# Attention scores on 64 partitions from batch 2 on, the missing rows moved by SBUF to SBUF copies, and GpSimd's value work placed half a group earlier

## The chip, the cores and the metric

The kernel runs on one core of one Trainium2 chip. The metric is the device time of one execution in microseconds (us), lower is better. "Span" is the time from the first to the last instruction of the one execution that was profiled; it is about 2 us below the device time of the same execution (329.5 and 331.33 us before).

## The reference, cut to what matters

```python
# 8 batches, 8 heads, 576 positions, head size 64; q, k, v are 0.1 * randn
def _attn_ref(q, k, v):
    q_d, k_d, v_d = (mean of each 4 neighbouring positions, for q, k and v)
    out_up = np.repeat(softmax(scale * q_d @ k_d.T) @ v_d, 4, axis=2)
    mask = np.abs(pos[:, None] - pos[None, :]) < 4
    scores = np.where(mask, scale * q @ k.T, -1e9)
    return out_up + softmax(scores) @ v

def _moe_ref(x, w_in, w_out):          # x: 4608 tokens x 512, 512 -> 2048 -> 512
    h = x @ w_in
    return (h * (1 / (1 + np.exp(-1.702 * h)))) @ w_out
```

So each batch has a narrow attention inside a band, an attention on pooled positions, and the sum of both goes through a large two-layer network.

## The kernel before: the parts that matter

The 4608 tokens go through the network in nine groups of 512. Group g runs on TensorE as 64 large matmuls with `w_in` and 64 with `w_out`; between fixed ones of them stand the small matmuls of the attention of batch g + 1. There are two score blocks to a batch (`qd` 0 and 1, four heads each), each followed by the scores on pooled positions. GpSimd makes what these blocks need: pooled q and k (`pool_qk`), values cast to bf16 (`prep_v`), pooled values (`prep_v4`). GpSimd also issues the loads of q, k and weights; the SyncE queue issues the value loads and the output stores.

```python
def prep_1(name, b, qd):               # VectorE transposes q or k, 576 columns as 18 x 32
    store, dst = {"k": (kf, kT), "q": (qf, qT)}[name]
    tt = work.tile([128, S, 2], BF16, ..., bufs=1)
    t32 = tt.rearrange("p t a -> p (t a)").bitcast(FP32)
    nc.vector.transpose(out=..., in_=store[b, qd].bitcast(FP32)...)   # pairs of bf16 as one fp32
    dst[b, qd] = tt

def scores(b, qd, barred=False):       # 80 matmuls a block, each on 32 partitions
    ...
    for i in range(5):
        for a in range(2):             # the two elements of a pair, summed in PSUM
            for par in range(2):
                for r in range(4):     # head
                    rows = slice(32 * r, 32 * r + 32)
                    nc.tensor.matmul(sp[r // 2][...],
                        lhsT=kT[b, qd][rows, k0 : k0 + 64, a],
                        rhs=qT[b, qd][rows, q0 : q0 + 60, a],
                        start=(a == 0 ...), stop=(a == 1 ...), tile_position=(32 * r, 64 * par))

for g in range(n_groups):              # what is prepared during group g
    b = g + 1
    ...
    elif b < B:
        if b > 2:
            load_v4(b)
        prep_qk(b, 0); pool_qk(b, 0)
        if b + 1 < B:
            for qd in range(NQ):
                load_qk(b + 1, qd)     # GpSimd issues the next batch's q and k
        prep_v(b, nc.gpsimd)
        if b + 1 < B:
            load_v(b + 1)
        prep_qk(b, 1); pool_qk(b, 1)
        prep_v4(b, nc.gpsimd)
    ...                                # then the attention steps and the group's matmuls
```

The transpose moves pairs of bf16 values. So a head's 64 features lie on 32 partitions, two to a partition, and a score needs two matmuls, one for each element `a` of the pair.

The softmax here doesn't subtract the row's maximum and nothing guards it: scores larger than these inputs give would overflow.

Of the kernel before, what the change touches and what calls it, by code (L numbers as in the profile page):

```python
# [8 lines left out]
FP32 = mybir.dt.float32  # L9
# [10 lines left out]
def kernel(  # L20
# [9 lines left out]
    nc = tc.nc  # L30
# [8 lines left out]
    inv_sqrt_d = 1.0 / math.sqrt(D)  # L39
    KSTART = (0, 56)  # L40
    QSTART = (0, 60)

    ctx.enter_context(
        tc.manual_schedule(engines={ET.PE, ET.Activation, ET.DVE, ET.Pool, ET.SP})
# [19 lines left out]
    eds = [persist.tile([128, 2, 464], BF16, name=f"ed{i}") for i in range(2)]  # L64
    v4 = persist.tile([128, 3, HP, 4 * D], FP32, name="v4")
    kdT = [persist.tile([128, 160, 2], BF16, name=f"kdT{i}") for i in range(NQ)]

    PA = [psum.tile([128, 2, 512], FP32, name=f"pa{i}") for i in range(3)]
    PM = [psum.tile([128, 512], FP32, name=f"pm{i}") for i in range(2)]
# [2 lines left out]
    def ps_tile(n=None):  # L72
        if n is None:
            n = turn["a"] % 3
            turn["a"] += 1
        return PA[n]
# [44 lines left out]
    def fill():  # L121
        nc.vector.memset(wz, 0.0)
        for t in kdT:
            nc.vector.memset(t[:, SD:160, :], 0.0)
        for t in vbs:
            nc.vector.memset(t[:, :, :, 64:65], 1.0)
        for t in vds:
            nc.vector.memset(t[:, :, :, 64:65], 4.0)
        for t in es:
            nc.vector.memset(t[:, :, 300:304], 1.0)  # L130
        for t in eds:
            nc.vector.memset(t[:, :, 432:464], 1.0)
# [122 lines left out]

    def prep_1(name, b, qd):
        store, dst = {"k": (kf, kT), "q": (qf, qT)}[name]
        tt = work.tile([128, S, 2], BF16, name=f"{name}T{qd}", tag=f"{name}T{qd}", bufs=1)
        t32 = tt.rearrange("p t a -> p (t a)").bitcast(FP32)
        nc.vector.transpose(  # L260
            out=t32.rearrange("p (i c) -> p c i", c=18),
            in_=store[b, qd].bitcast(FP32).rearrange("p (c d) -> p c d", c=18),
        )
        dst[b, qd] = tt

    def prep_qk(b, qd):
        prep_1("k", b, qd)
        prep_1("q", b, qd)

    def pool_qk(b, qd, names="kq"):  # L270
        for name, src in (("k", kT), ("q", qT)):
            if name not in names:
                continue
            sv = src[b, qd].rearrange("p (j f) a -> p j f a", f=4)
            t1 = work.tile([128, SD, 2, 2], FP32, name="pq", tag="pq")
            nc.gpsimd.tensor_tensor(  # L276
                out=t1, in0=sv[:, :, 0:2, :], in1=sv[:, :, 2:4, :], op=ALU.add
            )
            if name == "k":
                dst = kdT[qd][:, 0:SD, :]  # L280
            else:
                t = work.tile([128, SD, 2], BF16, name=f"qdT{qd}", tag=f"qdT{qd}", bufs=1)
                qdT[b, qd] = t
                dst = t
            nc.gpsimd.tensor_tensor(
                out=dst, in0=t1[:, :, 0, :], in1=t1[:, :, 1, :], op=ALU.add
            )

    def prep_v(b, eng, i=slice(0, 5), h=slice(0, H)):
        cp = eng.copy if eng is nc.scalar else eng.tensor_copy  # L290
        cp(out=vbs[b % 2][:, i, h, 0:D], in_=vf[b][:, i, h])  # L291
# [47 lines left out]

    def scores(b, qd, barred=False):  # L340
        sp = [ps_tile(), ps_tile()]
        if barred:
            bar_others(sp)
        for i in range(5):
            for a in range(2):
                for par in range(2):
                    for r in range(4):
                        rows = slice(32 * r, 32 * r + 32)
                        k0 = 114 * i + KSTART[par]
                        q0 = 114 * i + QSTART[par]  # L350
                        nc.tensor.matmul(  # L351
                            sp[r // 2][64 * par : 64 * par + 64, r % 2, 60 * i : 60 * i + 60],
                            lhsT=kT[b, qd][rows, k0 : k0 + 64, a],
                            rhs=qT[b, qd][rows, q0 : q0 + 60, a],
                            start=(a == 0 and not barred),
                            stop=(a == 1 or barred),
                            tile_position=(32 * r, 64 * par),
                            skip_group_check=barred,
                        )
        return sp  # L360

    def scores_d(b, qd, sd=None):
        sd = sd or ps_tile()
        bank = sd if sd is PM else [sd[:, u, :] for u in range(2)]
        for kc in range(3):
            for a in range(2):
                for r in range(4):
                    rows = slice(32 * r, 32 * r + 32)
                    j = r % 2
                    nc.tensor.matmul(  # L370
                        bank[r // 2][64 * j : 64 * j + 64, SD * kc : SD * kc + SD],
                        lhsT=kdT[qd][rows, 48 * kc : 48 * kc + 64, a],
                        rhs=qdT[b, qd][rows, :, a],
                        start=(a == 0), stop=(a == 1),
                        tile_position=(32 * r, 64 * j),
                    )
        return sd
# [325 lines left out]
    POS = [13, 16, 33, 42, 53, 62, 71]  # L703
    POS_0 = [16, 18, 27, 54, 68, 60, 76]
    VDP_0 = 52

    o, y, x = {}, {}, {}

# [93 lines left out]
    def loads_2():  # L802
        load_v(2)
        load_v4(2)

    for g in range(n_groups):
        b = g + 1
        if g == 0:
            prep_qk(1, 0)
            pool_qk(1, 0)  # L810
            prep_qk(1, 1)
            load_v(1, gate=after(w_out_bf[0:1, 0, 0:1], nc.vector))
            pool_qk(1, 1)
            nc.gpsimd.tensor_copy(
                out=w_out_bf[0:1, 8, 0:1], in_=vf[1][0:1, 3, 0, 0:1]
            )
            load_w_out(2)
            load_w_out(3)
            for i in range(5):
                prep_v(1, nc.gpsimd, i=slice(i, i + 1))  # L820
            for qd in range(NQ):
                load_qk(2, qd)
            loads_2()
        elif b < B:
            if b > 2:
                load_v4(b)
            prep_qk(b, 0)
            pool_qk(b, 0)
            if b + 1 < B:
                for qd in range(NQ):  # L830
                    load_qk(b + 1, qd)
            prep_v(b, nc.gpsimd)
            if b + 1 < B:
                load_v(b + 1)
            prep_qk(b, 1)
            pool_qk(b, 1)
            prep_v4(b, nc.gpsimd)
        steps = {}
        if b < B:
            for n, f in zip(POS if g else POS_0, attention(b, None if g else (1, 2))):  # L840
                steps.setdefault(n, []).append(f)
            if g == 0:
                steps.setdefault(VDP_0, []).append(lambda: prep_vd_pe(1, PA[2]))
        gT = new_gT() if g else gT0
        mm1(g, gT, steps, 0 if g else 6)
        mm2(g, gT, {n - 16: f for n, f in steps.items() if n >= 16})
# [30 lines left out]
```

## Time and profile before

| what | before |
|---|---|
| time, median of 3 runs | 329.46 us (328.81 to 330.97) |
| span of the profiled execution | 329.5 us |
| TensorE busy | 308.0 us, 93% |
| first score block of a steady batch, from a big matmul's start to the next one's | 1.47 us |
| second score block, the same | 1.76 to 1.90 us |
| group in which batch 2, 3, 4, 5, 6, 7 is prepared | 35.10, 33.71, 33.53, 33.39, 34.32, 33.39 us |

The last row is worked out from the trace: from the start of a group's first matmul with `w_in` to that of the next group.

First the page of the kernel before: span, busy time of the engines, then the span in 40 slices (tenths of busy time; PEclk is the granted TensorE clock in tenths, DMA the mean busy share of the 16 DMA engines), and the engines of the chain of waits that ended last.

```profile
span 329.5 us, 11220 instructions
PE 308.0 (93%) x4987; PEld 157.9 (48%) x5043; DVE 130.2 (40%) x215; ACT 184.1 (56%) x322; POOL 138.9 (42%) x168
PE   8767999789999999999999999998999999999995
PEclk9997999999999999999999999999999999999999
DMA  7999979999814991398339922993180110011011
PE 87%; issue 4%; SPq 3%; ACT 2%; DVE 2%; DMA 1%; DVEq 0%; ACTq 0%
```

TensorE bounds the kernel, and in this execution its clock never drops after the start-up (mean 0.995; other runs of the same kernel have means from 0.982).

Now the timeline of TensorE in the group of batch 2 (start, length, engine, line, operation, tiles, count).

```profile
79.42 0.84 PE L351 MATMUL pa<-qT,kT 32*64 32x60 bf16 x80
80.06 0.59 PE L370 MATMUL pa<-qdT,kdT 32*64 32x144 bf16 x24
80.59 2.76 PE L618 MATMUL pm<-xT,w_in_bf 128*128 128x512 bf16 x11
...
90.55 0.48 PE L431 MATMUL pa<-vd,ed 48*64 48x65 bf16 x18
```

L431 holds the products with the pooled values. L351 holds the band's scores, L370 the pooled ones; none of these waits. From 79.42 to 80.06 the 80 matmuls start 8 ns apart.

And the timeline of GpSimd in the same group, cut. L285 ends a pooled q or k, L291 is the cast of the values, L300 ends a pooled value.

```profile
73.03 0.67 POOL L285 TENSOR_TENSOR qdT<-pq 128x288 bf16<-128x288 f32 x1
...
75.78 2.36 POOL L291 CAST vb<-vf 128x2560 bf16<-128x2560 f32 x1
...
81.17 0.67 POOL L285 TENSOR_TENSOR qdT<-pq 128x288 bf16<-128x288 f32 x1
...
87.19 0.84 POOL L300 TENSOR_TENSOR vd<-v 112x256 bf16<-112x256 f32 x1
```

The first pooled q is ready at 73.7 us, 6 us before the scores want it, and the last pooled value at 88.0.

### The profile page before, as it was taken

The page shows a single profiled execution, that of the slowest core. Times are in us where ns is not written, and L with a number is a line of the kernel's source. Part 1 is how long each engine was busy: PE and PEld are TensorE (multiplying, and loading weights), DVE is VectorE, ACT ScalarE, POOL GpSimd, SP SyncE. Part 2 cuts the span into 40 slices and gives each one's busy share as a digit, 9 for nine tenths or more (in the row PEclk, how much of TensorE's full clock was granted, in tenths as well). Part 3 has the DMA queues.
Part 4 walks back from the last instruction along what each step waited for, and adds up shares of the span by engine and source line. Part 5 has one row for each costly group of instructions (what it writes and reads, how often), then busy time and mean ns, then how long its engine had stood idle before and what let it go on. Part 6 is the DMA issues. An engine that isn't in the chain of part 4 may idle for free.

```text
span 329.5 us, 11220 instructions
## 1 busy us (share of the span) xinstructions
PE 308.0 (93%) x4987; PEld 157.9 (48%) x5043; DVE 130.2 (40%) x215; ACT 184.1 (56%) x322; POOL 138.9 (42%) x168
## 2 busy tenths in 40 slices
PE   8767999789999999999999999998999999999995
PEld 3444455445554455455544555455444544444444
DVE  4870512770468036802771277225730560000000
ACT  2552773375936683667367746674566646415611
POOL 7890844049603970298029901990098000000000
PEclk9997999999999999999999999999999999999999
DMA  7999979999814991398339922993180110011011
GB/s 126 184 188 208 171 151 183 196 210 236 191 39 132 205 207 39 116 193 171 102 100 200 200 83 86 196 195 105 40 172 2 60 41 32 2 72 56 2 62 65
DMA packets 63552, 41.36 MB, mean 126 GB/s; under 512 B 44048, under 2 KB 54416, under 8 KB 63504
## 3 DMA queue, kind: packets, MB, share of 16 engines
q1 hardware_dynamic: 55056, 26.95, 35.8%
q0 software_dynamic: 8304, 13.63, 23.9%
q8 instruction: 39, 0.64, 0.9%
q14 instruction: 9, 0.07, 0.1%
q10 hardware_dynamic: 144, 0.07, 0.1%
HBM read 44.83 MB, written 9.44 MB: 165 GB/s over the span
## 4 chain that ended last, share of the span: by engine, by line
PE 87%; issue 4%; SPq 3%; ACT 2%; DVE 2%; DMA 1%; DVEq 0%; ACTq 0%
PE pm L618 35%; PE pm L674 33%; PE pa L351 3%; SPq L214 3%; PE pa L618 2%; PE pa L431 2%; PE pa L409 2%; PE pa L370 2%; PE pa L458 2%; PE pa L674 2%; DMA vf<-in_v_dram 1%; PE pm L689 1%; PE pa L484 1%; ACT vd L321 0%; PE pa L312 0%
## 5 line engine op out<-in xcount | busy, mean ns | idle before, releaser
L618 PE MATMUL pm<-xT,w_in_bf 128*128 128x512 bf16 x528 | 120.3, 380 | 1.4 <-DVE xT L561 0.7
L674 PE MATMUL pm<-w_out_bf,gT 128*128 128x512 bf16 x493 | 114.1, 379 | 5.4 <-issue 5.2
L629 ACT ACTIVATE gT<-pm 128x512 bf16<-128x512 f32 x136 | 81.0, 598 | 45.2 <-PE pm L618 45.2
L618 PEld LDWEIGHTS <-w_in_bf 128*128 128x128 bf16 x576 | 55.8, 98 | 68.4 <-issue 2.5
L674 PEld LDWEIGHTS <-gT 128*128 128x128 bf16 x560 | 51.7, 98 | 59.5 <-issue 0.2
L276 POOL TENSOR_TENSOR pq<-kT 128x576 f32<-128x576 bf16 x16 | 18.5, 1157 | 105.0 <-DVE kT L260 96.1
L395 DVE TENSOR_TENSOR es<-es,mask 128x600 bf16<-128x600 bf16 x28 | 20.6, 749 | 92.0 <-ACT es L381 91.2
L659 ACT ACTIVATE osb<-pm 128x512 f32<-128x512 f32 (+2 forms) x35 | 20.7, 592 | 40.2 <-PE pm L674 36.1
L534 ACT COPY od<-pa 128x384 f32<-128x384 f32 (+1 forms) x56 | 18.4, 412 | 32.4 <-DVE y L444 18.7
L444 DVE TENSOR_TENSOR y<-pa,rc 128x896 bf16<-128x896 f32 x32 | 34.9, 1092 | 1.1
L555 DVE TENSOR_TENSOR xT<-pa,od 128x570 bf16<-128x570 f32 x28 | 21.1, 753 | 12.0 <-ACT od L534 11.9
L381 ACT ACTIVATE es<-pa 128x600 bf16<-128x600 f32 x32 | 19.8, 668 | 7.0 <-PE pa L351 6.8
L297 POOL TENSOR_TENSOR v<-v 112x512 f32<-112x512 f32 x18 | 22.8, 1265 | 0.0
L661 DVE TENSOR_SCALAR osb<-pm 128x128 f32<-128x128 f32 x1 | 0.3, 292 | 55.3 <-ACT osb L659 55.3
L260 DVE STREAM_TRANSPOSE kT<-kb 128x576 f32<-128x576 f32 x16 | 20.0, 1249 | 2.0 <-DMA kb<-in_k_dram 2.0
L260 DVE STREAM_TRANSPOSE qT<-qb 128x576 f32<-128x576 f32 x16 | 19.8, 1239 | 0.9 <-DMA qb<-in_q_dram 0.7
L276 POOL TENSOR_TENSOR pq<-qT 128x576 f32<-128x576 bf16 x16 | 18.4, 1148 | 0.0
L291 POOL CAST vb<-vf 128x2560 bf16<-128x2560 f32 (+1 forms) x11 | 17.6, 1618 | 0.0
L442 DVE RECIPROCAL rc<-pa 128x14 f32<-128x14 f32 x32 | 7.7, 240 | 21.7 <-PE pa L431 21.7
L351 PE MATMUL pa<-qT,kT 32*64 32x60 bf16 x1280 | 14.0, 203 | 1.5 <-issue 1.5
L351 PEld LDWEIGHTS <-kT 32*64 32x64 bf16 x1280 | 11.8, 104 | 6.7 <-issue 5.5
L300 POOL TENSOR_TENSOR vd<-v 112x256 bf16<-112x256 f32 x18 | 13.7, 759 | 1.4
(90 smaller groups left out, 247.0 us busy)
## 6 DMA issues: line engine op xcount, KB each, us to landing
vf<-in_v_dram SPq DMA_DIRECT2D x80, 128.0 KB, 4.7
out_dram<-osb SPq DMA_DIRECT2D x35, 256.0 KB, 2.1
v<-in_v_dram SPq DMA_DIRECT2D x36, 192.0 KB, 6.1
kb<-in_k_dram POOLq DMA_DIRECT2D x16, 288.0 KB, 6.8
qb<-in_q_dram POOLq DMA_DIRECT2D x16, 288.0 KB, 7.1
w_out_bf<-in_moe_w_out_dram POOLq DMA_DIRECT2D x4, 512.0 KB, 12.1
w_in_bf<-in_moe_w_in_dram POOLq DMA_DIRECT2D x2, 512.0 KB, 5.7
w_in_bf<-in_moe_w_in_dram POOLq DMA_DIRECT2D x1, 1024.0 KB, 10.7
```

The lines of the kernel that those rows point to most:

```text
L260: nc.vector.transpose(out=t32.rearrange("p (i c) -> p c i", c=18), in_=store[b, qd].bitcast(FP32).rearrange("p (c d) -> p c d", c=18),)
L276: nc.gpsimd.tensor_tensor(out=t1, in0=sv[:, :, 0:2, :], in1=sv[:, :, 2:4, :], op=ALU.add)
L297: eng.tensor_tensor(out=t1[0:112], in0=x[:, :, 0:2, :], in1=x[:, :, 2:4, :], op=ALU.add)
L351: nc.tensor.matmul(sp[r // 2][64 * par : 64 * par + 64, r % 2, 60 * i : 60 * i + 60], lhsT=kT[b, qd][rows, k0 : k0 + 64, a], rhs=qT[b, qd] ...
L381: nc.scalar.activation(out=es[2 * qd + u][:, :, 0:300], in_=sp[u][:, :, 0:300], func=AF.Exp, scale=inv_sqrt_d,)
L395: nc.vector.tensor_tensor(out=ev, in0=ev, in1=mask, op=ALU.mult)
L444: nc.vector.tensor_tensor(out=y, in0=ov[:, :, :, 0:D], in1=rc.to_broadcast([128, 2, 7, D]), op=ALU.mult,)
L555: eng.tensor_tensor(out=sub(xT[hp], t0 + 3, (57, 2), (114, 5), (1, 57)), in0=sub(x, 3, (509, 2), (57, 5), (1, 57)), in1=sub(od, 3, (57, 2) ...
L618: nc.tensor.matmul(acc, lhsT=w_in_bf[:, dmc, ffc * 128 : (ffc + 1) * 128], rhs=xT[dmc][:, g * TG : g * TG + TG], start=(dmc == 0), stop=(d ...
L629: nc.scalar.activation(out=gT[:, ffc, :], in_=acc, func=AF.Silu, scale=GELU_SCALE)
L659: eng.activation(out=osb, in_=ap, func=AF.Copy, scale=1.0 / GELU_SCALE)
L674: nc.tensor.matmul(ops[t], lhsT=gT[:, ffc, t * 128 : (t + 1) * 128], rhs=w_out_bf[:, ffc, :], start=(ffc == 0), stop=(ffc == n_ffc - 1),)
```

## The change

The intent is to halve the score matmuls. From batch 2 on, q and k are transposed twice, and four copies to each tensor, from SBUF to SBUF on the SyncE queue, move 32 partitions and shift by one element, so that the second elements of the pairs stand on the other 32 partitions of a pair of heads. A head's 64 features are then on 64 partitions, and one matmul does what two did. Pooling on GpSimd reads the result, so it waits for the copies too. To give GpSimd room, the value work of batches 3 to 7 is done during the group before or at the start of its own; in batch 2 it stays behind the q and k sums.

```diff
+    ROWS64 = 2
 def prep_1(name, b, qd):
+        n = 2 if b >= ROWS64 else 1
+        tt = work.tile([128, 2, S, 2], BF16, ..., bufs=1)
+        for x in range(n):
+            ... nc.vector.transpose(out=(half x of tt), in_=(as before))
+        if n == 2:
+            for x in range(2):
+                f = tt[:, x].rearrange("p t a -> p (t a)")
+                for r in range(2):
+                    src = 64 * r + 32 * x
+                    to = 64 * r + 32 * (1 - x)
+                    nc.sync.dma_start(
+                        out=f[to : to + 32, 0 : 2 * S - 1], in_=f[src : src + 32, 1 : 2 * S]
+                    )
 def pool_qk(b, qd, names="kq"):
+            if b >= ROWS64:
+                ... (sums over element 0 of both halves; k goes to a new tile kdP)
 def scores(b, qd, barred=False):
+        if b >= ROWS64:
+            ... 40 matmuls, rows = slice(64 * u, 64 * u + 64), start=True, stop=True
+            return sp
 def scores_d(b, qd, sd=None):
+        if b >= ROWS64:
+            ... 12 matmuls on 64 rows
+    V4 = 34
+    def next_v4(b):
+        load_v4(b)
+        prep_v4(b, nc.gpsimd)
 for g in range(n_groups):
         elif b < B:
-            if b > 2:
-                load_v4(b)
+            if g > 1:
+                prep_v(b, nc.gpsimd)
             prep_qk(b, 0)
             pool_qk(b, 0)
             if b + 1 < B:
                 for qd in range(NQ):
                     load_qk(b + 1, qd)
-            prep_v(b, nc.gpsimd)
+            prep_qk(b, 1)
+            pool_qk(b, 1)
+            if g == 1:
+                prep_v(b, nc.gpsimd)
+                prep_v4(b, nc.gpsimd)
             if b + 1 < B:
                 load_v(b + 1)
-            prep_qk(b, 1)
-            pool_qk(b, 1)
-            prep_v4(b, nc.gpsimd)
...
+            if g and b + 1 < B:
+                steps.setdefault(V4, []).append(lambda b=b: next_v4(b + 1))
```

More of the change, by code (lines that the diff above doesn't have):

```diff
@@ L66 @@
     kdT = [persist.tile([128, 160, 2], BF16, name=f"kdT{i}") for i in range(NQ)]
+    kdP = [persist.tile([128, 2, 160], BF16, name=f"kdP{i}") for i in range(NQ)]
     PA = [psum.tile([128, 2, 512], FP32, name=f"pa{i}") for i in range(3)]
@@ L124, in fill @@
             nc.vector.memset(t[:, SD:160, :], 0.0)
+        for t in kdP:
+            nc.vector.memset(t[:, :, SD:160], 0.0)
         for t in vbs:
@@ L257, in prep_1 @@
         store, dst = {"k": (kf, kT), "q": (qf, qT)}[name]
-        tt = work.tile([128, S, 2], BF16, name=f"{name}T{qd}", tag=f"{name}T{qd}", bufs=1)
-        t32 = tt.rearrange("p t a -> p (t a)").bitcast(FP32)
-        nc.vector.transpose(
-            out=t32.rearrange("p (i c) -> p c i", c=18),
-            in_=store[b, qd].bitcast(FP32).rearrange("p (c d) -> p c d", c=18),
-        )
-        dst[b, qd] = tt
+        n = 2 if b >= ROWS64 else 1
+        tt = work.tile([128, 2, S, 2], BF16, name=f"{name}T{qd}", tag=f"{name}T{qd}", bufs=1)
+        for x in range(n):
+            t32 = tt[:, x].rearrange("p t a -> p (t a)").bitcast(FP32)
+            nc.vector.transpose(
+                out=t32.rearrange("p (i c) -> p c i", c=18),
+                in_=store[b, qd].bitcast(FP32).rearrange("p (c d) -> p c d", c=18),
+            )
[7 more added lines that the diff above has]
+                        out=f[to : to + 32, 0 : 2 * S - 1], in_=f[src : src + 32, 1 : 2 * S]
+                    )
+        dst[b, qd] = tt if n == 2 else tt[:, 0]
     def prep_qk(b, qd):
@@ L273, in pool_qk @@
                 continue
+            if b >= ROWS64:
+                sv = src[b, qd].rearrange("p x (j f) a -> p (x j) f a", f=4)[:, :, :, 0]
+                t1 = work.tile([128, 2 * SD, 2], FP32, name="pq", tag="pq", bufs=1)
+                nc.gpsimd.tensor_tensor(
+                    out=t1, in0=sv[:, :, 0:2], in1=sv[:, :, 2:4], op=ALU.add
+                )
+                if name == "k":
+                    dst = kdP[qd][:, :, 0:SD]
+                else:
+                    dst = work.tile([128, 2, SD], BF16, name=f"qdT{qd}", tag=f"qdT{qd}", bufs=1)
+                    qdT[b, qd] = dst
+                t1 = t1.rearrange("p (x j) f -> p x j f", x=2)
+                nc.gpsimd.tensor_tensor(
+                    out=dst, in0=t1[:, :, :, 0], in1=t1[:, :, :, 1], op=ALU.add
+                )
+                continue
             sv = src[b, qd].rearrange("p (j f) a -> p j f a", f=4)
-            t1 = work.tile([128, SD, 2, 2], FP32, name="pq", tag="pq")
+            t1 = work.tile([128, SD, 2, 2], FP32, name="pq", tag="pq", bufs=1)
             nc.gpsimd.tensor_tensor(
@@ L341, in scores @@
         sp = [ps_tile(), ps_tile()]
+        if b >= ROWS64:
+            for j in range(2):
+                for i in range(5):
+                    for par in range(2):
+                        for u in range(2):
+                            rows = slice(64 * u, 64 * u + 64)
+                            k0 = 114 * i + KSTART[par]
+                            q0 = 114 * i + QSTART[par]
+                            nc.tensor.matmul(
+                                sp[u][64 * par : 64 * par + 64, j, 60 * i : 60 * i + 60],
+                                lhsT=kT[b, qd][rows, j, k0 : k0 + 64, 0],
+                                rhs=qT[b, qd][rows, j, q0 : q0 + 60, 0],
+                                start=True, stop=True,
+                                tile_position=(64 * u, 64 * par),
+                            )
+            return sp
         if barred:
@@ L363, in scores_d @@
         sd = sd or ps_tile()
+        if b >= ROWS64:
+            for kc in range(3):
+                for j in range(2):
+                    for u in range(2):
+                        rows = slice(64 * u, 64 * u + 64)
+                        nc.tensor.matmul(
+                            sd[64 * j : 64 * j + 64, u, SD * kc : SD * kc + SD],
+                            lhsT=kdP[qd][rows, j, 48 * kc : 48 * kc + 64],
+                            rhs=qdT[b, qd][rows, j, :],
+                            start=True, stop=True,
+                            tile_position=(64 * u, 64 * j),
+                        )
+            return sd
         bank = sd if sd is PM else [sd[:, u, :] for u in range(2)]
```

## The prediction

> **What bounds it now.** TensorE. The page's busy table has PE at 308.0 of 329.5 us, and the chain of waits is 87% PE instructions; the two big matmul groups take 234 us. Between two big matmuls stand attention blocks. In the timeline a big matmul starts 0.216 us after the last; across the first score block of a batch (80 score and 24 pooled-score matmuls on 32 partitions) the step is 1.47 us, across the second 1.76 to 1.90 us. So a pair costs about 2.9 us. Inside, 80 scores take 0.64 to 0.85 us from start to start, 24 pooled ones 0.37 us: only four different tiles hold these, 6 rounds of 60 ns. The value matmuls, already on 64 partitions, take 9 ns each.
>
> **What the change removes.** In batches 2 to 7, 12 blocks, 52 matmuls of 104. Estimate from the rates above: 40 x 9 ns = 0.36 us, and three rounds of 60 ns = 0.18 us. A block saves 0.45 to 0.6 us: about 6 us, all of it on the critical path. That is just short of 2%.
>
> **What it adds.** 24 transposes of 1.08 us on VectorE, per group in an idle stretch (107 to 119 us of the trace); harmless. 96 DMAs of 74 KB on the SyncE queue, estimated 0.35 to 0.45 us of issue each and about 2 us to landing (the output stores took 2.0). GpSimd's sums keep 576 and 288 elements (1.15 and 0.67 us) but now wait for a DMA as well as a transpose. In the steady groups scores come 11.2 us after the group's start; transposes, DMAs and sums of the first half should take about 10: slack over 1 us. Doing the value sums half a group earlier pays for this on GpSimd.
>
> **Where it is given back: batch 2.** There the value work is still behind the q/k sums. The SyncE queue reuses eight DMA semaphores, so a DMA waits for the eighth before it. Batch 2's first kT copy so waits for a value load that landed at 73.7 us, the qT copies for output stores that landed at 76.2 to 77.8. I expect kT copies landed at 78, qT at 79.5 to 80, the q sum ready at 81.4 instead of 73.64. GpSimd then has the same 14.4 us of work as before (four loads, second q/k sums, the 2.36 us cast, three value sums): done at 95.8, where it was 88.0. PE wants the last pooled values at about 89.8. So PE loses about 6 us in this group: 1.5 to 2 us before its first pooled scores, 4 or more before the pooled value matmuls. A wait that long may also drop the clock: [...] this trace shows 0.5 for 3.41 us after 2.9 us of idle at 23.5. That would add 1 to 1.7 us. Later groups should recover and show only the gain.
>
> **Sum.** 329.5 - 6 + 6 + 1.5 = 331.0 us; range 326 to 335.5. Faster by over 2%: 0.06; within 2%: 0.85; slower by over 2%: 0.09.
>
> **What would show it.** Steps across score blocks of batches 3 to 7 near 1.0 and 1.2 us, and a group near 33 us instead of 34 (right: gain); PE idle 5 to 7 us at 79 to 97 us, released by GpSimd's sums (right: loss); no other PE wait over 1 us in later groups.
>
> **What would make it wrong.** Copies landing faster, or GpSimd's strided sums cheaper: no loss, 323 to 325 us. Copies landing in 4 us or more beside the loads: 1 to 2 us of wait in each group, 336 us or more. Score matmuls bound by loading weights, not by count: half the gain.

The sum: 329.5 - 6 + 6 + 1.5 = 331.0 us, and the 1.5 is an estimate from the trace of the kernel before, 2.87 us of idle up to 26.41 us and then 3.41 us at half rate (27.27 to 30.69), of which half is 1.7. Two other statements can be read there too. SyncE's 153 DMAs use eight semaphores in turn, and 131 of them first wait for the one that they then use. The 24 pooled scores start in six groups of four, about 65 ns from group to group (80.09 to 80.41 us).

## The result, and the profile after

| | before | after |
|---|---|---|
| time, median of 4 runs | 330.0 us (328.81 to 330.97) | 346.53 us (344.53 to 349.16) |
| span of the profiled execution | 329.5 us | 342.7 us |
| batch 2's group | 35.10 us | 49.04 us |
| groups of batches 3 to 7 | 33.71, 33.53, 33.39, 34.32, 33.39 us | 34.02, 33.99, 33.98, 33.17, 32.47 us |
| the two groups after | 27.63, 31.38 us | 27.63, 31.38 us |

The change made the kernel slower: the ratio is 1.0507, with a 95% interval of 1.0427 to 1.0588. Ratios here and below are the mean time of one kernel's fast runs over the mean of the other's fast runs of the same rounds, so they are not quite the ratio of the medians that are quoted. Executions over 1.5% slower than the fastest of the same kernel are left out of the means.

The prediction of 331.0 us and its range up to 335.5 were wrong. The table of groups says where: batch 2's group is 13.94 us longer, and batches 3 to 7 together are 0.71 us shorter (168.34 before, 167.63 after). The sum is 13.2 us, the whole difference of the two spans.

The page after, the same parts as before:

```profile
span 342.7 us, 10264 instructions
PE 307.6 (90%) x4363; PEld 154.5 (45%) x4419; DVE 156.9 (46%) x241; ACT 183.8 (54%) x322; POOL 140.1 (41%) x168
PE   8768998896939898999899989999999999999995
PEclk9998999998778999999999999999999999999999
DMA  7999789895859259875996599859964010011012
PE 50%; DMA 13%; DVE 12%; SPq 8%; issue 6%; POOL 5%; ACT 4%; DVEq 0%; POOLq 0%; ACTq 0%
```

Three things are new. PE has holes in slices 10 and 12 (77 to 86 us and 94 to 103 us), and PEclk falls to 7 and 8 in slices 10 to 13. The DMA row loses its low slices: the copies filled the gaps that the DMA engines had. The chain of waits is now only half TensorE, and DMA, VectorE and the SyncE queue stand in it with a third.

The windows view by group (stretch, its length, then busy time with the number of instructions for each engine, the granted clock, the DMA share and GB/s), first before, batches 2 and 3:

```profile
67.08:102.18 35.10, 33.30 (x594) 17.04 (x600) 17.43 (x27) 21.73 (x39) 17.52 (x19) 1.00 0.74 161
102.18:135.89 33.71, 32.80 (x594) 16.91 (x600) 16.34 (x25) 20.95 (x36) 17.52 (x19) 1.00 0.68 142
```

and after, the same two batches:

```profile
67.09:116.13 49.04, 37.57 (x491) 18.20 (x497) 23.58 (x31) 21.62 (x39) 25.33 (x26) 0.86 0.72 168
116.13:150.14 34.01, 31.74 (x490) 15.99 (x496) 19.70 (x29) 20.95 (x36) 12.95 (x16) 1.00 0.82 173
```

In batch 3's group TensorE has 104 matmuls and 1.06 us of busy time less, as intended, yet the group is not shorter. The DMA engines went from 0.68 to 0.82 there. In batch 2's group the mean clock is 0.86: the clock records show 13.65 us at half rate (82.30 to 89.13 and 99.36 to 106.19).

TensorE's timeline after, batch 2, answers the lines of before; the bracket holds the idle time before the line and what released it:

```profile
83.59 0.57 PE L416 MATMUL pa<-qdT,kdP 64*64 64x144 bf16 x12 [2.08 <-POOL qdT L301]
84.93 4.40 PE L678 MATMUL pm<-xT,w_in_bf 128*128 128x512 bf16 x10 [0.22 <-issue]
...
98.35 0.23 PE L491 MATMUL pa<-vd,ed 48*64 48x65 bf16 x4 [2.00 <-POOL vd L331]
100.37 0.27 PE L491 MATMUL pa<-vd,ed 48*64 48x65 bf16 x4 [1.80 <-POOL vd L331]
102.39 0.38 PE L491 MATMUL pa<-vd,ed 48*64 48x65 bf16 x10 [1.75 <-POOL vd L331]
```

TensorE waits 2.08 us for pooled q, then runs ten big matmuls in 4.40 us (before, eleven took 2.76), and later waits 5.55 us in all for the three pooled values, one after the other.

GpSimd's timeline after, batch 2, cut:

```profile
82.88 0.67 POOL L301 TENSOR_TENSOR qdT<-pq 128x288 bf16<-128x288 f32 x1
...
85.09 0.57 POOL L198 DMA_DIRECT2D qb<-in_q_dram  x1
...
91.43 1.15 POOL L292 TENSOR_TENSOR pq<-qT 128x576 f32<-128x576 bf16 x1 [3.86 <-DMA qT<-qT]
...
93.38 2.56 POOL L322 CAST vb<-vf 128x2560 bf16<-128x2560 f32 x1
...
101.61 0.73 POOL L331 TENSOR_TENSOR vd<-v 112x256 bf16<-112x256 f32 x1
```

The first pooled q is there at 83.5 instead of 73.7. Then GpSimd issues the loads of batch 3's q and k, and the second half's sum waits until 91.43 for its copies. Everything of the value work stands behind that sum. The last pooled value is ready at 102.3 instead of 88.0.

The chain of waits through that place, and through the same place of batch 3's group (start, length, what):

```profile
85.13 6.15 DMA qT<-qT
91.44 1.14 POOL pq L292
...
93.43 2.50 POOL vb L322
...
102.39 0.38 PE pa L491 x10
...
127.01 4.50 DMA qT<-qT
...
134.13 1.42 POOL pq L292
...
136.33 0.38 PE pa L416 x12
```

In batch 2 a copy of the second half took 6.15 us from issue to the sum. In batch 3 the copy issued at 127.01 took 4.85 us to land by the trace, against 2.0 us for the copies of the first half. Between it and the sum at 134.13 the chain goes over ScalarE and VectorE instructions, and the profile names a VectorE mask multiply (L455) as what released the sum. The semaphores in the trace say otherwise: that sum waits only for the transposes, long done, and for the semaphores of four copies. The last copy was issued at 127.60, the last packets of 2,302 bytes, a row of these copies, end at 133.4, and GpSimd's wait for that copy's semaphore ends at 134.0. It was a DMA. Here the wait costs TensorE 1.36 us; the four groups of batches 3 to 6 have 1.36, 1.13, 1.41 and 0.57 us of it, always before L416, and batch 7, which has no following batch to load, has none and takes 32.47 us.

### The profile page after: what moved, and what is told of

Read it like the earlier page. It is cut to its first block, busy times and chain, and to the rows that moved or that the text cites. A ratio compares the mean times of both kernels' runs of the same rounds, so it can differ in the third digit from the quotient of the medians.

```text
span 342.7 us, 10264 instructions
## 1 busy us (share of the span) xinstructions
PE 307.6 (90%) x4363; PEld 154.5 (45%) x4419; DVE 156.9 (46%) x241; ACT 183.8 (54%) x322; POOL 140.1 (41%) x168
## 3 DMA queue, kind: packets, MB, share of 16 engines
q1 hardware_dynamic: 59664, 34.02, 42.3%
## 4 chain that ended last, share of the span: by engine, by line
PE 50%; DMA 13%; DVE 12%; SPq 8%; issue 6%; POOL 5%; ACT 4%; DVEq 0%; POOLq 0%; ACTq 0%
PE pm L734 23%; PE pm L678 14%; DMA qT<-qT 8%; SPq L276 6%; DVE qT L266 4%; DVE kT L266 4%; DMA out_dram<-osb 4%; SPq L218 3%; PE pa L678 2%; PE pa L491 2%; PE pa L469 2%; POOL pq L292 2%; DMA vf<-in_v_dram 2%; PE pa L734 1%; ACT od L594 1%
## 5 line engine op out<-in xcount | busy, mean ns | idle before, releaser
L678 PE MATMUL pm<-xT,w_in_bf 128*128 128x512 bf16 x528 | 122.6, 385 | 1.6 <-DVE xT L621 0.7
L734 PE MATMUL pm<-w_out_bf,gT 128*128 128x512 bf16 x493 | 115.4, 382 | 5.6 <-issue 5.4
L455 DVE TENSOR_TENSOR es<-es,mask 128x600 bf16<-128x600 bf16 x28 | 20.5, 748 | 70.8 <-ACT es L441 70.0
L266 DVE STREAM_TRANSPOSE kT<-kb 128x576 f32<-128x576 f32 x28 | 33.0, 1244 | 2.2 <-DMA kb<-in_k_dram 1.7
L266 DVE STREAM_TRANSPOSE qT<-qb 128x576 f32<-128x576 f32 x28 | 32.8, 1239 | 1.1 <-DMA qb<-in_q_dram 1.1
L292 POOL TENSOR_TENSOR pq<-kT 128x576 f32<-128x576 bf16 x12 | 14.0, 1165 | 33.3 <-DMA kT<-kT 31.7
L292 POOL TENSOR_TENSOR pq<-qT 128x576 f32<-128x576 bf16 x12 | 14.0, 1167 | 19.4 <-DMA qT<-qT 11.9
L491 PE MATMUL pa<-vd,ed 48*64 48x65 bf16 x640 | 12.4, 196 | 6.3 <-POOL vd L331 5.6
L447 ACT ACTIVATE ed<-pa 128x864 bf16<-128x864 f32 x15 | 13.6, 906 | 0.8 <-PE pa L416 0.7
```

What stands on the lines that cost most here:

```text
L266: nc.vector.transpose(out=t32.rearrange("p (i c) -> p c i", c=18), in_=store[b, qd].bitcast(FP32).rearrange("p (c d) -> p c d", c=18),)
L292: nc.gpsimd.tensor_tensor(out=t1, in0=sv[:, :, 0:2], in1=sv[:, :, 2:4], op=ALU.add)
L455: nc.vector.tensor_tensor(out=ev, in0=ev, in1=mask, op=ALU.mult)
L678: nc.tensor.matmul(acc, lhsT=w_in_bf[:, dmc, ffc * 128 : (ffc + 1) * 128], rhs=xT[dmc][:, g * TG : g * TG + TG], start=(dmc == 0), stop=(d ...
L734: nc.tensor.matmul(ops[t], lhsT=gT[:, ffc, t * 128 : (t + 1) * 128], rhs=w_out_bf[:, ffc, :], start=(ffc == 0), stop=(ffc == n_ffc - 1),)
```

## The experiments

Theory A, after the result: the loss is batch 2's, where copies that land late push the value work of the same batch back; the rest of the change is worth what was predicted. Rivals: the new order on GpSimd costs by itself (B); the 96 small issues on one queue are the limit (C). Letters beyond C in the expectations are later forms of the question whether the DMA traffic costs by itself, also where nobody waits for a copy; each says what it expects. Every kernel ran four times, beside seven runs of the kernel before on the same chip; their medians in the four sessions were 331.85, 331.12, 330.11 and 331.68 us. Group lengths are those of the one profiled execution, so small differences between them are not proven. "Waits" are idle times of TensorE.

### 1. Only the order on GpSimd

```diff
-    ROWS64 = 2
+    ROWS64 = 99
```

> Only the new order of GpSimd's work; no batch uses 64 rows, so there is no second transpose and no copy. Theory A (the copies of the second half of q share the DMA engines with the q/k loads of the next batch, land late, and GpSimd's value work of batch 2 stands behind them): without copies nothing is late, 328 to 331 us. Rival B (the new order by itself costs, because in batch 2 the value cast now stands behind the second q/k sums): 335 us or more.

Measured: 332.35 us (332.04 to 332.88), ratio 1.0014 (0.9959 to 1.0068). Groups 36.23, 33.51, 33.39, 35.03, 33.99, 33.39 us. The order by itself costs nothing that can be seen. B falls.

### 2. Everything but the copies

The scores are wrong: half of each matmul's rows belong to another head. The result still passes the comparison, because inputs this small give nearly flat softmaxes, so passing says nothing here.

```diff
-        if n == 2:
+        if n == 3:          # never: no copies
             for x in range(2):
```

> The change without its 96 copies (wrong result on purpose: rows that a copy would fill keep the doubled transpose). Everything else is there: 24 added transposes, 624 fewer matmul pairs, the new order. Theory A and any theory that puts the loss on the copies: the pure gain, 12 blocks at 0.5 us, 323 to 325 us. Rival B, or a loss by the added transposes on VectorE: 330 us or more.

Measured: 329.45 us (326.83 to 330.73), ratio 0.9911 (0.9842 to 0.998). Batch 2's group took 33.97 us with no half clock; where nothing waits a group takes 32.46 us against 33.39 before. So the transposes are harmless, and the gain of 0.93 us a group is real: the 13.94 us and all the waits for GpSimd come with the copies. But the median gained 2.4 us, less than the 5.6 us of six such groups. Two groups of the profiled run hold waits of 1.37 and 1.63 us, which end with no semaphore; experiments 10 and 14 come back to these.

### 3. The next batch's q and k loads behind the pooling

```diff
             prep_qk(b, 0)
             pool_qk(b, 0)
+            prep_qk(b, 1)
+            pool_qk(b, 1)
             if b + 1 < B:
                 for qd in range(NQ):
                     load_qk(b + 1, qd)
-            prep_qk(b, 1)
-            pool_qk(b, 1)
```

> The change, with the q/k loads of the next batch issued after the second q/k sums of this one instead of before. Theory A: the second-half q copies land in 2 to 3 us instead of 5 to 6; in batch 2 GpSimd gets 4 us earlier, the waits of 0.6 to 1.4 us before the second pooled scores of batches 3 to 6 go: 334 to 338 us. Rival C (the cost is SyncE's own issue, 0.6 us for each copy and eight semaphores in turn): unchanged, 343 us or more.

Measured: 347.36 us (347.13 to 351.36), ratio 1.0489 (1.0416 to 1.0562). The expectation of A was missed by 9 us. Its mechanism did show. GpSimd in batch 2, cut:

```profile
84.68 1.15 POOL L292 TENSOR_TENSOR pq<-qT 128x576 f32<-128x576 bf16 x1 [0.70 <-DMA qT<-qT]
...
97.04 0.73 POOL L331 TENSOR_TENSOR vd<-v 112x256 bf16<-112x256 f32 x1
```

The sum that waited 3.86 us for its copies now waits 0.70, and the waits before L416 in batches 3 to 7 are gone but for 0.16 us. But the value work still stands behind all four sums, ends at 97.8 (this execution runs about 2 us earlier, so the gain is about 2 us), TensorE still waits 5.48 us for it, and the clock is at half for the same 13.65 us: batch 2's group is 48.12 us. The later groups took 35.04, 36.81, 36.00, 32.92 and 32.82 us: the loads, moved away from the copies, now run with the value loads, and new waits without a semaphore appear. Moving loads is no cure; it moves the collision.

### 4. Batch 2's value work ahead of its q and k sums

```diff
-            if g > 1:
-                prep_v(b, nc.gpsimd)
+            prep_v(b, nc.gpsimd)
+            if g == 1:
+                prep_v4(b, nc.gpsimd)
             prep_qk(b, 0)
...
-            if g == 1:
-                prep_v(b, nc.gpsimd)
-                prep_v4(b, nc.gpsimd)
```

> The change, with the cast and pooled values of batch 2 ahead of its q/k sums on GpSimd, as in the later batches. If the batch 2 loss is value work that stands behind late copies (theory A, second part), the 8.2 us step before the value matmuls of batch 2 falls to about 1.4 us and the second clock drop goes: 334 to 338 us. If the loss of batch 2 is the first wait alone with the clock that it drops (rival D): 342 us or more.

Measured: 337.79 us (335.68 to 339.24), ratio 1.0168 (1.0104 to 1.0232). TensorE's instructions are the same as after the change. Batch 2's group fell from 49.04 to 40.25 us, with 3.41 us at half clock; no wait for pooled values is left. What is left there are two waits for pooled q:

```profile
84.23 0.58 PE L416 MATMUL pa<-qdT,kdP 64*64 64x144 bf16 x12 [2.12 <-POOL qdT L301]
...
94.49 0.38 PE L416 MATMUL pa<-qdT,kdP 64*64 64x144 bf16 x12 [1.46 <-ACT es L441]
```

The profile puts the second down to ScalarE, but GpSimd's second pooled q, which had waited 4.34 us for its copies, was ready only at 94.44.

So the order of batch 2 is worth 8.8 us, and this was as expected.

### 5. The copies from batch 3 on

```diff
-    ROWS64 = 2
+    ROWS64 = 3
```

> The change with 64 rows from batch 3 on. If the loss is batch 2's (copies that come late behind value loads and stores, value work behind them, half clock after it: its group took 49.0 us against 35.1), this group returns to 35 to 36 us and all else stays: 328.5 to 331 us. If the loss moves to batch 3 with the first use of copies (theory E: any first batch of copies costs it), 336 us or more.

Measured: 336.25 us (333.01 to 338.4; one of the four slow), ratio 1.0122 (1.0049 to 1.0195). Against the change that is 10 us less, and batch 2's group fell from 49.04 to 38.69 us, so most of the loss there came with batch 2's copies. But the expectation was missed twice. The group did not return to 35 to 36 us. With no copy in it, it has a wait of 1.82 us that no semaphore ends, and after that 3.41 us at half clock:

```profile
95.67 0.29 PE L491 MATMUL pa<-vd,ed 48*64 48x65 bf16 x10 [1.82 <-issue]
```

And by A the rest should have been at or below the kernel before, and it is about 4 us above (172.21 against 168.34 us for these five groups): batches 3 to 6 have 1.95, 0.91, 1.36 and 1.81 us of waiting for pooled q, and the last of these is followed by 3.41 us at half clock. The groups of batches 3 to 7 took 34.60, 34.17, 34.74, 36.24 and 32.46 us.

### 6. From batch 3 on, with the later loads

This joins the edits of 3 and 5.

> 64 rows from batch 3 on and the q/k loads of the next batch after the second q/k sums. Later loads took the wait before the second pooled scores away (1.1 to 1.4 us a group) but in the run with them other waits came, 1.5 to 2.7 us each, that no semaphore ends and that follow a landing of PE's own instructions by 1.3 to 1.6 us. If such fetches come late because the q/k loads now meet the value loads (theory F), groups stay at 34 us or more: 330 us or more. If they were chance, groups fall to 32.5 to 33 us: 325 to 327 us.

Measured: 337.87 us (336.33 to 345.43, that one slow), ratio 1.0181 (1.0137 to 1.0224). The waits for pooled q are nearly gone (0.26 us in one group) and the time is no better: waits without a semaphore that add up to 2.65, 1.38, 1.68, 1.71 and 2.18 us stand in the groups of batches 2 to 6. (The profile puts 0.90 us of the 1.68 down to ScalarE; experiment 14 shows why it is counted here.)

### 7 and 8. Half as many copies of twice the size, from batch 2 and from batch 3

```diff
+        if name == "k":
+            pair[qd] = work.tile([128, 2, 2, S, 2], BF16, ...)   # k and q in one tile
+        tt = pair[qd][:, 0 if name == "k" else 1]
-        if n == 2:
+        if n == 2 and name == "q":
...
-                        out=f[to : to + 32, 0 : 2 * S - 1], in_=f[src : src + 32, 1 : 2 * S]
+                        out=f[to : to + 32, :, 0 : 2 * S - 1], in_=f[src : src + 32, :, 1 : 2 * S]
```

> The change with k and q of a half in one tile and one copy for both: 48 copies of 144 KB instead of 96 of 72 KB, the same bytes. Rival C (SyncE's issue, 0.6 us a copy, bounds when copies land): the second half's copies are issued 2 to 3 us earlier, ahead of the q/k loads, the waits before the second pooled scores go in batches 3 to 6, and batch 2 gains 3 us or more: 334 to 340 us. If bytes on the DMA engines bound them: unchanged, 344 us or more.

> Both: 64 rows from batch 3 on and one copy for k and q. If batch 2 and SyncE's issue are the whole loss, five batches keep their gain of 0.95 us each: 324 to 327 us. If bytes bound the copies, as from3: 328.5 to 331 us.

Measured: 347.12 us (346.18 to 351.5), ratio 1.0473 (1.0437 to 1.051), and from batch 3 on 340.79 us (339.81 to 342.95), ratio 1.03 (1.0258 to 1.0343). Half the issues brought no better time from batch 2 on. Batch 2's group did get 3.8 us shorter (45.28 us), as C said, but the waits for pooled q in batches 3 to 6 stayed (0.92, 1.05, 0.67 and 1.04 us), and batch 6's group took 37.62 us, with a wait of 2.38 us without a semaphore and half clock. From batch 3 on it was 4.5 us worse than experiment 5: k's sums wait for q's transposes too, and now even batch 7, with no loads beside it, waits 1.04 us. So fewer issues do not cure the loss. C is not excluded cleanly, because the edit also makes k's copies wait for q's transposes. Both expectations for the second kernel were missed.

### 9. Without the loads of pooled values

The kernel of experiment 6 with `load_v4` left out for batches 3 to 7; its values are wrong (relative error 0.12).

```diff
     def next_v4(b):
-        load_v4(b)
         prep_v4(b, nc.gpsimd)
```

> The kernel from3_later with the v4 loads of batches 3 to 7 left out (wrong result on purpose: these batches pool batch 2's values): PE's instructions are the same to the last, 6 MB of traffic on the DMA engines are gone. Theory F (PE's instruction fetches come late because the DMA engines are full): the fetch waits of 1.4 to 2.7 us in its groups shrink, groups of batches 3 to 7 fall to 32.5 to 33.3 us, 326 to 331 us. Rival G (where the 16 KB instruction blocks happen to end decides, not the traffic): the same waits stay, 336 us or more.

Measured: 335.36 us (329.26 to 335.98). One run counts as fast, the profiled one as slow, so there is no ratio. It did show that the waits without a semaphore are in the same places: 1.66, 2.11 and 2.16 us, before the same counted instructions of TensorE as in experiment 6. Something in the instruction stream fixes the place. But not all is fixed: of the four other waits in the steady groups of experiment 6 (0.83, 1.82, 0.90 and 0.78 us), one fell to 0.72 us and three are gone or under 0.45 us. So three places speak for G and four for F, in one execution of each, and the median lies between the two forecasts.

### 10. The copies' traffic, with nobody reading it

The kernel of experiment 1, plus the change's copies for batches 2 to 7 into an unused half tile.

```diff
+        if b >= 2:
+            f, h = (tt[:, x].rearrange("p t a -> p (t a)") for x in range(2))
+            for x in range(2):
+                for r in range(2):
+                    ... nc.sync.dma_start(out=h[to : to + 32, ...], in_=f[src : src + 32, ...])
```

> The kernel order_only (32 rows everywhere, 332.35 us) with the 96 copies of the change made into a half tile that nothing reads, so no sum and no matmul waits for them: only their traffic and SyncE's issue are added. Theory F: the traffic alone costs, by fetch waits and late loads, 336 to 342 us. Rival H (the copies cost only because GpSimd and PE wait for them): 330 to 334 us.

Measured: 336.02 us (333.51 to 338.12), ratio 1.0157 (1.0069 to 1.0245), against 1.0014 without the copies. The window of batch 3 (columns as above), first without the copies, experiment 1:

```profile
102.01:135.52 33.51, 32.61 (x594) 16.78 (x600) 14.36 (x23) 20.95 (x36) 17.19 (x19) 1.00 0.67 143
```

then with them:

```profile
100.72:137.11 36.39, 33.86 (x602) 17.05 (x601) 15.16 (x25) 20.95 (x36) 21.80 (x24) 1.00 0.86 191
```

Copies that no sum and no matmul waits for cost about 4.7 us (the difference of the ratios, 1.43% of 330; the two intervals just fail to meet, so its size is uncertain by some 3 us). TensorE's program is the same in both; the trace of experiment 1 lacks 56 of TensorE's records, which is why its count here is lower. The DMA share of batch 3's group goes from 0.67 to 0.86, and that group holds a wait of 2.47 us which ends with no semaphore:

```profile
126.44 0.28 PE L500 MATMUL pa<-vd,ed 48*64 48x65 bf16 x8 [2.47 <-issue]
```

Batch 5's group has three such waits, of 0.83, 1.02 and 1.01 us. After the start-up TensorE waits for no sum of GpSimd here. So copies are a cost of their own, apart from anything that waits for them. The run adds their bytes and SyncE's issues together and does not tell the two apart.

### 11. Only the second score block on 64 partitions

Half as many copies, in the order of the kernel before.

```diff
+    def wide(b, qd):
+        return b >= ROWS64 and qd == 1
...
-        n = 2 if b >= ROWS64 else 1
+        n = 2 if wide(b, qd) else 1
(the same in pool_qk, scores and scores_d; value work and loads as in the kernel before, but load_v behind the copies)
```

> 64 rows only in the second half (qd 1) of batches 2 to 7, GpSimd's order as before the change: 12 fewer transposes and 48 fewer copies than the change, which have 8 us more to land. If slack and traffic decide, it keeps most of 6 blocks at 0.5 us and loses nothing in batch 2: 327 to 330 us. If any copies cost more than they give here: 332 us or more.

Measured: 347.93 us (344.37 to 350.07, that one slow), ratio 1.0489 (1.0403 to 1.0575). A clear miss. With the order of before, the value sums of every batch stand behind sums that wait for copies, and so the groups of batches 2 to 6 do what batch 2 does in the change. TensorE's waits for pooled values:

```profile
PE pa L494 <- POOL vd L334: 12.3, 8, 2.0
```

Of the 24 copies whose landing is recorded, 20 land 5.2 to 6.7 us after issue, beside loads, and four groups have 3.41 us at half clock.

### 12 and 13. The same with the value work ahead, from batch 2 and from batch 3

Half the copies as in 11, the order of the change, and in batch 2 the value work before the second half's sums:

```diff
             prep_qk(b, 1)
-            pool_qk(b, 1)
             if g == 1:
                 prep_v(b, nc.gpsimd)
                 prep_v4(b, nc.gpsimd)
+            pool_qk(b, 1)
```

> 64 rows only in the second half as in second_half, but with the change's order: value work a half group ahead from batch 3 on, and in batch 2 before the second q/k sums. In second_half the copies landed 5 to 7 us after issue and GpSimd's value sums stood behind them, so PE waited 2 to 3.5 us for pooled values in each group. If that is the cause, these waits go and 6 blocks keep 0.4 us or more: 328 to 332 us. If copies cost by their traffic whatever stands behind them: 335 us or more.

> The same from batch 3 on, batch 2 with 32 rows: within 2 us of second_ahead if batch 2 is cured there (328 to 332 us); 4 us or more faster if batch 2 still pays.

Measured: 330.41 us (330.25 to 330.65), ratio 0.9962 (0.9914 to 1.0011), and from batch 3 on 331.41 us (330.73 to 333.56), ratio 1.0003 (0.9942 to 1.0064). Both as expected, and both the same as before within the interval. GpSimd in batch 2 of the first, cut:

```profile
74.89 2.37 POOL L325 CAST vb<-vf 128x2560 bf16<-128x2560 f32 x1
...
82.61 0.73 POOL L334 TENSOR_TENSOR vd<-v 112x256 bf16<-112x256 f32 x1
83.30 1.15 POOL L295 TENSOR_TENSOR pq<-kT 128x576 f32<-128x576 bf16 x1
```

The k copies take 6.6 to 6.7 us to land here, yet the sum of k does not wait for them, because 8.4 us of value work stands between; the sum of q waits 0.63 us for the last q copy. It is the order of the value work with its loads, not the speed of a copy, that makes the difference of 17.5 us to experiment 11 (of another session, whose kernel before was 1.6 us faster). No TensorE wait for pooled values is left, only one of 1.36 us for pooled q in batch 2; the groups took 35.24, 32.99, 34.82, 34.45, 33.02 and 32.99 us, and there is no half clock in them. Where nothing waits, half the change gives a little under half the gain (33.39 to 32.99). Two groups lose it again to waits of 1.54 and 1.28 us, which end with no semaphore.

### 14. The same kernel with TensorE's instructions shifted

The waits without a semaphore stood at fixed places. Counted over all of TensorE's records in the trace (matmuls, weight loads and its few semaphore instructions), those of experiment 6, the start-up included, come at 449, 961, 3009, 3265, 4289, 4545, 5313, 6081 and 7105: all leave 193 when divided by 256. The DMA queue that the profile calls "instruction" moves packets of 16 KB (0.64 MB in 39 packets before). Those 39 packets stand beside 10,043 records of TensorE in the same trace, about 257 to a packet. With the remainders this points to one packet for each 256 instructions; below, such a stretch is called a block. So the kernel of experiment 6 got 64 tiny matmuls, 128 instructions with their weight loads, before its first score block:

```diff
     warm(19)
+    t = pm_tile()
+    for _ in range(64):
+        nc.tensor.matmul(t[0:32, 0:8], lhsT=wz[:, 0:32], rhs=wz[:, 0:8], start=True, stop=True)
     make_mask()
```

> from3_later with 64 tiny matmuls (128 PE instructions) put into the wait for the first load. In the traces of from3_later and of no_v4 the waits that no semaphore ends stand before the same PE instructions, 1024 and 1792 (multiples of 256) apart. If PE waits at the ends of its 16 KB instruction blocks (256 instructions), the waits now stand at other lines, 128 instructions earlier in the program, at the same count from its start; the time may move by some us either way. If something else at these lines makes PE wait, they stay at the same lines.

Measured: 332.70 us (332.11 to 333.71), ratio 1.0041 (0.9979 to 1.0103). Adding instructions to the engine that bounds the kernel brought the ratio from 1.0181 down to 1.0041. Two of the waits in TensorE's timeline, first of experiment 6:

```profile
196.68 0.28 PE L491 MATMUL pa<-vd,ed 48*64 48x65 bf16 x8 [1.71 <-issue]
232.79 2.73 PE L734 MATMUL pm<-w_out_bf,gT 128*128 128x512 bf16 x6 [2.18 <-issue]
```

then with the shift:

```profile
201.97 0.21 PE L528 MATMUL pa<-ident,y 48*64 48x48 bf16 x3 [1.84 <-issue]
230.63 0.22 PE L469 MATMUL pa<-vb,es 64*64 64x65 bf16 x2 [1.16 <-issue]
```

The waits stand at other lines but at the same remainder (2241, 4289, 4545, 6593 and 7361 all leave 193). So they come at ends of blocks of 256 instructions, and which stretch of the program has the end decides what it costs. In experiment 3, for example, TensorE resumes 1.4 us after such a packet has ended (packet 137.25 to 138.18, TensorE at 139.60).

The kept traces of experiments 5 to 14, in which no record of TensorE is missing, show more. Their instruction queue moves one 16 KB packet for each block after the first. TensorE never passes a block's start sooner than 1.2 us after the end of its packet (counted in the same way, never sooner than 1.26 us in the trace before and 1.35 us in the trace after), and at all 64 block ends where it stands still for over 0.5 us it goes on 1.2 to 1.8 us after that end. At these places the packet itself took 1.2 us in the median, but it began only 0.5 to 5.0 us after TensorE had begun the block before. So it matters how fast TensorE runs through a block: of 93 blocks that it ran through in under 5 us, those with many small attention matmuls, 46 ended in such a wait, of 161 that took over 7 us none. The kernel before has the wait too: the 2.87 us of idle in its start-up that the prediction quotes stand at the same instruction as the wait at 961.

What sets the moment at which a packet begins was not found. In experiments 1 and 10, with the same program, the packets took the same in the mean (1.15 and 1.19 us in the groups of batches 2 to 7). At three of the four places where batches 3 and 5 wait in experiment 10 they began about 2 to 3 us later than in experiment 1; at one place of batch 2, where experiment 1 waits, 2.2 us earlier. That traffic on the DMA engines delays them is therefore supported, not shown. All this also means that differences of a per cent or so between two of these kernels can come from where their blocks end.

## Why the prediction was wrong

| term | predicted | measured in the profiled executions |
|---|---|---|
| fewer score matmuls, six groups | -6 us | -5.6 us (0.93 a group where nothing waits) |
| waits in batch 2's group, more than before | +6 us | +9.7 us (TensorE idle 11.47 us, before 1.80) |
| half clock in batch 2's group | +1.5 us | about +5.2 us (estimate, the rest: 49.04 - 35.10 + 0.93 - 9.7) |
| waits in the groups of batches 3 to 7 | 0 | +3.9 us (4.65 of gain, 0.71 left) |
| sum | +1.5 us | +13.2 us |

Two of the measured terms are remainders, so that the sum fits is no check of them.

What bounds the kernel was right, and so was the gain. The step over a first score block fell from 1.47 to 0.95 us, and a group without waits from 33.39 to 32.47 us. 40 matmuls start 9 ns apart where 80 started 8 ns apart, so the count decides, as the prediction had it.

The transposes were rightly called harmless (experiment 2), and the order of GpSimd's work by itself as well (experiment 1). A copy of the first half lands in 2.0 us as predicted, 1.97 to 2.05 us in most groups. The issue of one mostly took 0.53 to 0.60 us on the queue, not the 0.35 to 0.45 predicted; halving the number of issues did not mend the time (experiment 7), so this is unlikely to be what counted.

The mechanism of batch 2 was right, its size was not. The prediction said "GpSimd then has the same 14.4 us of work as before" and "done at 95.8". The first pooled q came 2.1 us later than it said (83.5, not 81.4); the one k copy of the first half whose landing is recorded took 3.4 us, not 2. The rest of the error is a wait that the prediction left out: it costed the copies of the first half only, and the second half's q copies, issued beside the loads that GpSimd then sent off, took 6 us and stopped GpSimd for 3.86 us, with all the value work behind it. It was done at 102.3. The clock term "1 to 1.7 us" came from a single half window after one wait. Here a wait of 2.08 us and a row of three of 1.75 to 2.00 us each came with 6.83 us at half rate (from 82.30 and from 99.36). The length of a wait alone did not decide it: waits of 1.82 and 1.81 us in experiment 5 were followed by 3.41 us at half clock, the one of 2.47 us in experiment 10 was not (clock 1.00 in that group).

So in batch 2 two terms of the sum were too small: the waits (6 us, measured 9.7) and the half clock (1 to 1.7 us, about 5.2). The step that failed in kind is "Later groups should recover and show only the gain." They recover, but batches 3 to 6 give back 0.57 to 1.41 us each to the copies of the second half, which run beside the next batch's loads, with the first half's slack of over 1 us costed and the second half's not costed at all. The prediction had this among its risks ("Copies landing in 4 us or more beside the loads: 1 to 2 us of wait in each group, 336 us or more"), and gave it too small a weight: the second half's copies whose landing the trace records took 3.7 to 5.0 us in these groups, and the waits were near or below the low end of what it says. How the DMA engines share their time between the queues was not measured beyond this: in the trace after, from 130 to 133.4 us packets of these copies and of the q and k loads start in a mixed order, and the copies are the ones with someone waiting.

Behind both is one omission. The prediction counted the DMA engines as nearly free. They were 0.68 busy in a steady group and are 0.82 with the copies, and copies that nobody waits for cost about 1.4% (experiment 10), most visibly as waits of TensorE that no semaphore ends (2.47 us in batch 3's group of experiment 10). Without the copies the change gains 0.9% (experiment 2); the version with half of the copies and the value work ahead of them ties with the kernel before (experiment 12). No version here clearly beats it.

What stays open: how much of each kernel's time is from late instruction blocks and how much from the copies themselves, since the edits also move where the blocks end, and what sets the moment at which a block's packet begins.

## What to carry to other kernels

Before trading matmuls for copies, look at the DMA share of the stretch in which the copies would run: where it was 0.72 and 0.82 in the mean of a group here (batches 2 and 3 after), the second half's q copies took 3.7 to 6.1 us to land beside the loads, against 2.0 in batch 7's group without them, and copies that nobody read still cost about 1.4%. Put nothing with a deadline behind an instruction that waits for such a copy on the same engine: on GpSimd the cast stood behind the sum that waited until 91.43 us and began at 93.38 (75.78 before). Copies of the second half cost nothing where 8 us of other work stood before their reader, and 17 us where the work stood behind it. When a wait shows no semaphore, count instructions to see whether it falls on a block of 256, look for a packet of the instruction queue that ended 1.2 to 1.8 us before TensorE went on, and shift the program before believing a difference of a per cent. Of the blocks of 256 that TensorE ran through in under 5 us, those with many small matmuls and weight loads, 46 of 93 ended in such a wait here.
